# Attention with beacons, then a soft mixture of experts: weight transfers cut into smaller packets, V's conversions and copies moved to other pairs, beacon copies spread over engines

## The chip, the cores and the metric

The kernel runs on one core of one Trainium2 chip. The metric is the device time of one launch in microseconds, the median of several runs. A profile of one execution is read beside it; its times count from the start of the profiled span. Engines are named as in the profile: PE (TensorE matmul), PEld (its weight load), DVE (VectorE), ACT (ScalarE), POOL (GpSimd), SP (SyncE, which only issues transfers here).

## The reference

Queries, keys and values have shape 8 x 8 x 576 x 64 (batches, heads, rows, width), float32. Each head has 16 more keys and values, the beacons, which every query sees; the other keys are causal.

```python
k_all = np.concatenate([beacon_k, k], axis=2)
v_all = np.concatenate([beacon_v, v], axis=2)
scores = scale * np.matmul(q, k_all.transpose(0, 1, 3, 2))
causal[:, Nb:] = np.triu(np.ones((S, S), dtype=bool), k=1)
a = softmax(np.where(causal, -1e9, scores))
attn = np.matmul(a, v_all)
```

The heads of a row are put side by side to x (4608 x 512), and a soft mixture of 8 experts with 4 slots each follows:

```python
logits = x @ phi                                  # 4608 x 32
d = softmax of logits over the 4608 rows
slot_input = d.T @ x                              # 32 slots x 512
slot_out[e] = relu(slot_input[e] @ w1[e]) @ w2[e] # w1 512 x 1024, w2 1024 x 512
out = softmax of logits over the 32 slots @ slot_out
```

## The kernel before

**Pairs.** Two heads are one pair; four pairs are one batch, and the kernel walks 32 pairs, n = 0 to 31. For each pair it has a list of words (`order` and `lists`, lines 544 to 560), written out by hand, and `do` (L571) emits each word's instructions. Every engine takes its instructions in that order, so the lists set the order of the work on all of them. `order[n % 4]` is the list of the steady pairs; below, "list 4k" means one with n % 4 = 0.

**Words.** `S0` to `S3` score a pair in four steps (L366 on PE, the exponential at L373 on ACT, masks at L357 on POOL; `S0` belongs to the next pair). `M` is the mask of the first step (L383, DVE). `A0` and `A1` attend for the pair before, one head each (L396, PE); with `A1`, DVE takes reciprocals (L404) and writes xb (L405), which frees the accumulators for the next `A0`. `Qa Qb Ka Kb` transpose q and k of the next two pairs (L345 on PE, copied by DVE at L347); `T` words do the same for a single pair (L330, L332). `X0 X12 X34` transpose xb, `L0 L1` make logits (L457, exponential at L461), `D` transposes the dispatch weights (L496; dT copied at L498 to L500), and `SI` adds a batch to the slot inputs (L525, added to siq at L529). `BC` and `BT` cast and transpose the beacons of batches 1 to 7 (L305, L310, copies at L320).

**V.** A batch's values come by two transfers of 128 partitions x 2 rows (`load_r`) in packets of 512 bytes, a small one of beacon values into the first of these tiles (`load_bv`), and two for the last rows (`load_vl`). `c0 c1` convert them to 16 bits (L411, POOL in steady lists), `cl` the last rows (L428, four POOL instructions), and `d0 d1` copy the first 64 partitions to a second, padded tile vd (L421, DVE), which `attend` reads. The tiles vh and vd exist twice, by batch.

**Loads.** SP issues q, k and V in program order, q and k six pairs ahead into five buffers each, in packets of 2304 bytes. The weights are issued by POOL (L191), cast from 32 to 16 bits on the way: 27 whole pieces of 1 MB (read) and ten halves. `worder` takes w1 and w2 of experts 0 to 3 first, then w1 of experts 4 to 7, then their w2. How many pieces have been issued by pair n is `want(n)` (L628); the issue stands ahead of `S0`, and in the last pair ahead of `D`. A whole piece is 256 rows of w1 or 512 rows of w2; partition p reads two or four neighbouring rows in one run of 8192 bytes. So a tile's partitions hold every second row of x's width (or every fourth of the hidden width), and the operands that meet the weights are taken with the same stride (`every2`, L503, and `turn`, L736).

**Tail.** After the last pair the slot sums, layer 1 (L725), relu (L732, L734), `turn` (L741, copied at L744 into a padded tile that POOL clears at L702), and layer 2 (L752) follow. Only then are the outputs made (L792, scaled at L794 and L797) and stored.

Of the kernel before, what the change touches and what calls it, by code (L numbers as in the profile page):

```python
# [17 lines left out]
def kernel(  # L18
# [153 lines left out]
    NPC = 4 * E  # L172
    NV = NW + 3
# [7 lines left out]
    def load_w(x):  # L181
        if x < NV:
            m, hs = worder[x], (0, 1)
            t = (wh if x < NW else vrp).tile([P, 2048], F16, name="w", tag="w" if x < NW else "vr")
        else:
            m, hs = worder[NV + (x - NV) // 2], ((x - NV) % 2,)
            t = qkp.tile([P, J * P], F16, name="wx", tag=homes[x - NV])
        e, r = divmod(m, 4)
        w = moe_w1[e, r * 256:(r + 1) * 256] if r < 2 else moe_w2[e, (r - 2) * 512:(r - 1) * 512]
        src = w.rearrange("(p s) f -> p (s f)", p=P)  # L190
        nc.gpsimd.dma_start(out=t[:, 0:1024 * len(hs)],  # L191
                            in_=src[:, 1024 * hs[0]:1024 * (hs[-1] + 1)])
        for i, h_ in enumerate(hs):
            wv[(m, h_)] = t[:, 1024 * i:1024 * (i + 1)]
# [83 lines left out]
    EG = 4  # L278
# [28 lines left out]
    def beacon_t(b0, b1, copy=nc.vector.tensor_copy):  # L307
# [6 lines left out]
        for lo, hi in [(0, 2)] if b0 == 0 else [(2, 3), (3, M - 1), (M - 1, M)]:  # L314
            for r in range(2):
# [4 lines left out]
                copy(out=dst[64 * r:64 * r + 64, 2 * lo:2 * hi, :].rearrange(  # L320
# [103 lines left out]
    def cast_vl(b):  # L424
        t = vl.pop(b)
        for r in range(2):
            for i in range(2):
                nc.gpsimd.tensor_copy(  # L428
                    out=vh[b % 2][64 * i:64 * i + UE, 4, H // 2 * r:H // 2 * (r + 1), 0:D],
                    in_=t[64 * r:64 * r + UE, :, D * i:D * i + D])  # L430
# [71 lines left out]

    def every2(t):  # L503
        lo = 2 * P * (t // 2) + t % 2
        return slice(lo, lo + 2 * P - 1, 2)

    def si_piece(b):
        sp = ps_tr.tile([P, NDC, NSL], FP, name="tr", tag="tr")
        for t in range(NDC):
            for i in range(NCH):  # L510
# [3 lines left out]
                    xb[b % 2][0:m, POS[i], :, :].rearrange("p h d -> p (h d)")[:, every2(t)],  # L514
# [17 lines left out]
    def si_turn():  # L532
        sp = ps_tr.tile([P, NDC, NSL], FP, name="tr", tag="tr")
        for t in range(NDC):
            nc.tensor.matmul(sp[:, t, :], siq[:, every2(t)], slc[:, :],
                             start=True, stop=True)
# [7 lines left out]
    order = ["S1 A0 L1 M S2 Qa Qb S3 A1 Ka S0", "S1 D A0 SI M S2 Kb S3 A1 X0 c0 S0",  # L544
             "S1 A0 M S2 Qa Qb S3 A1 X12 d0 c1 S0", "S1 A0 L0 M S2 Ka Kb S3 A1 X34 d1 cl S0"]
# [25 lines left out]
    def do(n, w):  # L571
# [13 lines left out]
        elif w == "BC":  # L585
            beacon_cast(1, B, nc.scalar.copy)
        elif w == "BT":
            beacon_t(1, B, nc.scalar.copy)
# [16 lines left out]
        elif w[0] == "c" or w[0] == "d":  # L605
# [4 lines left out]
            elif w == "cl":  # L610
                cast_vl(vb)
# [24 lines left out]
    beacon_t(0, 1, nc.scalar.copy)  # L636
# [197 lines left out]
```

## Time and profile before

| | |
|---|---|
| median of 3 runs | 205.14 us (203.96 to 206.57) |
| profiled execution, whole time | 206.35 us |
| its span | 204.6 us, mean granted clock 0.939 |
| PE / DVE / ACT / POOL busy | 161.9 / 145.3 / 130.7 / 115.5 us |
| packets of SP's queue | 34375, 38.87 MB, 56.2% of 16 engines' span |
| packets of POOL's queue | 5328, 16.78 MB written, 42.5% |
| whole weight piece, issue to landing | 8.3 us median |
| first weight issue, last weight landing | 29.3 us, 175.8 us |
| layer 2 ends, outputs begin | 176.3 us, 177.7 us |

A packet's size in the profile is what it writes: a weight packet of 4096 bytes has read 8192. A row of instruction groups reads: line, engine, operation, output <- inputs, shapes, count, then busy time and mean duration, and the engine's idle time before them with what ended it. In a timeline the first two columns are start and length in us, neighbouring instructions of one kind are merged with their count (x2), and the bracket at the end is the idle time before and its releaser.

### The profile page before, as it was taken

To read this page: it belongs to the slowest core of one execution; us is meant where nothing else is said; L and a number is where in the kernel's file an instruction comes from. 1 tells how busy PE (TensorE), PEld (TensorE's weight loads), DVE (VectorE), ACT (ScalarE), POOL (GpSimd) and SP (SyncE) were. 2 spreads that over 40 slices of the span, in tenths; PEclk is the share of its full clock that TensorE was granted. 3 is DMA by queue.
4 is the path that set the end of the run, shared out by engine and by line. 5 is a ranking of instruction groups with operands and counts; after the bars stand their busy time and mean duration, and the time that the engine had idled before them with its cause. 6 is when DMAs were issued, how large, how long until landed. Compare 5 with 4: busy or idle time off the path is not lost.

```text
span 204.6 us, 6942 instructions
## 1 busy us (share of the span) xinstructions
PE 161.9 (79%) x2893; PEld 110.5 (54%) x2893; DVE 145.3 (71%) x294; ACT 130.7 (64%) x191; POOL 115.5 (56%) x278
## 2 busy tenths in 40 slices
PE   2669774899999989999898999589999999888000
PEld 2337562667667657667566675367677764332000
DVE  4665589587988989788998898469796624499100
ACT  3574883678788778878777787628868211399000
POOL 7996269347976759754983885169974650000000
PEclk9999999589999999999999999859999999999855
DMA  6999999988999899999999999999999999199995
GB/s 194 311 343 352 333 339 236 243 268 193 321 235 283 285 272 287 239 319 316 304 255 291 338 260 285 257 314 206 214 215 212 186 205 191 39 354 420 416 418 213
DMA packets 39735, 56.09 MB, mean 274 GB/s; under 512 B 4127, under 2 KB 24343, under 8 KB 39703
## 3 DMA queue, kind: packets, MB, share of 16 engines
q1 hardware_dynamic: 34375, 38.87, 56.2%
q0 software_dynamic: 5328, 16.78, 42.5%
q8 instruction: 22, 0.36, 0.6%
q14 instruction: 10, 0.08, 0.1%
HBM read 62.98 MB, written 9.44 MB: 354 GB/s over the span
## 4 chain that ended last, share of the span: by engine, by line
PE 33%; DVE 32%; DMA 11%; POOL 7%; issue 5%; ACT 4%; POOLq 0%; DVEq 0%; SPq 0%
PE av L396 10%; DMA qf<-in_q_dram 8%; DVE xb L405 8%; DVE qT L347 6%; PE sc L366 5%; DVE kT L347 5%; DVE osb L797 4%; DMA kf<-in_k_dram 3%; PE tr L345 3%; ACT ex L373 3%; DVE vd L421 3%; PE tr L457 3%; PE av L752 2%; PE tr L525 1%; DVE siq L529 1%
## 5 line engine op out<-in xcount | busy, mean ns | idle before, releaser
L373 ACT ACTIVATE ex<-sc 128x928 f16<-128x928 f32 (+2 forms) x128 | 106.5, 868 | 34.6 <-PE sc L366 27.5
L357 POOL TENSOR_SCALAR_AFFINE_SELECT ex<-ex 128x256 f16<-128x256 f16 x128 | 52.0, 426 | 38.5 <-ACT ex L373 33.4
L396 PEld LDWEIGHTS <-ex 128*128 128x128 f16 (+1 forms) x960 | 44.1, 110 | 18.2 <-issue 16.0
L366 PE MATMUL sc<-qT,kT 64*64 64x128 bf16 (+3 forms) x640 | 47.5, 270 | 4.9 <-ACT ex L373 2.5
L396 PE MATMUL av<-vh,ex 128*128 128x65 f16 x819 | 44.9, 203 | 0.8 <-POOL ex L357 0.7
L366 PEld LDWEIGHTS <-kT 64*64 64x64 bf16 (+1 forms) x640 | 17.9, 106 | 21.3 <-issue 9.9
L396 PE MATMUL av<-vd,ex 128*128 128x130 f16 x126 | 22.9, 232 | 6.3 <-DVE xb L405 6.0
L405 DVE TENSOR_TENSOR xb<-av,r 128x640 f16<-128x640 f32 (+1 forms) x32 | 26.1, 814 | 1.1
L347 DVE COPY qT<-tr 128x640 bf16<-128x640 bf16 (+1 forms) x24 | 17.5, 770 | 8.2 <-PE tr L345 8.2
L411 POOL CAST vh<-vr 128x1024 f16<-128x1024 f32 x15 | 15.8, 1053 | 8.9 <-DMA vr<-in_beacon_v_dram 8.9
L347 DVE COPY kT<-tr 128x640 bf16<-128x640 bf16 (+1 forms) x24 | 18.0, 771 | 3.8 <-PE tr L345 3.6
L383 DVE TENSOR_TENSOR ex<-ex,fmask 128x672 f16<-128x672 f16 x32 | 17.7, 554 | 0.9 <-ACT ex L373 0.6
L794 ACT ACTIVATE osb<-fp,rc 128x512 f32<-128x512 f32 (+1 forms) x19 | 12.0, 665 | 6.6 <-PE fp L792 6.3
L191 POOL DMA_DIRECT2D w<-in_moe_w_dram x27 | 15.0, 557 | 0.0
L428 POOL CAST vh<-vl 48x256 f16<-48x256 f32 x32 | 14.0, 438 | 1.1
L421 DVE COPY vd<-vh 64x1040 f16<-64x1040 f16 x16 | 13.9, 870 | 0.2
L345 PE MATMUL tr<-idb,kf 128*64 128x128 bf16 x216 | 10.4, 227 | 3.0 <-DVE qT L347 3.0
L797 DVE TENSOR_SCALAR osb<-fp,rc 128x512 f32<-128x512 f32 x18 | 12.3, 745 | 0.6 <-PE fp L792 0.6
L792 PE MATMUL fp<-soh,eLh 128*128 128x512 f16 (+1 forms) x37 | 10.8, 371 | 2.2 <-DVE soh L777 0.6
L345 PE MATMUL tr<-idb,qf 128*64 128x128 bf16 x216 | 9.4, 230 | 2.8 <-DMA qf<-in_q_dram 2.8
L442 PE MATMUL tr<-idh,xb 128*128 128x128 f16 (+1 forms) x140 | 11.4, 223 | 0.2 <-DVE kT L332 0.2
L447 DVE COPY xT<-tr 128x512 f16<-128x512 f16 (+1 forms) x21 | 10.5, 502 | 0.4 <-PE tr L442 0.4
(110 smaller groups left out, 176.7 us busy)
## 6 DMA issues: line engine op xcount, KB each, us to landing
w<-in_moe_w_dram POOLq DMA_DIRECT2D x27, 512.0 KB, 8.3
qf<-in_q_dram SPq DMA_DIRECT2D x32, 288.0 KB, 7.5
kf<-in_k_dram SPq DMA_DIRECT2D x32, 288.0 KB, 6.1
out_dram<-osb SPq DMA_DIRECT2D x16, 512.0 KB, 6.0
vr<-in_v_dram SPq DMA_DIRECT2D x15, 512.0 KB, 6.2
wx<-in_moe_w_dram POOLq DMA_DIRECT2D x10, 256.0 KB, 10.2
vl<-in_v_dram SPq DMA_DIRECT2D x16, 96.0 KB, 6.4
out_dram<-osb SPq DMA_DIRECT2D x3, 256.0 KB, 2.6
```

Of the source, the lines that this page charges most:

```text
L191: nc.gpsimd.dma_start(out=t[:, 0:1024 * len(hs)], in_=src[:, 1024 * hs[0]:1024 * (hs[-1] + 1)])
L345: nc.tensor.transpose(tp[64 * r:64 * r + 64, j - j0, :], ts[r][:, j, :].bitcast(BF)[:, 1::2], idb[:, :])
L347: nc.vector.tensor_copy(out=dst[:, :, Nb:Nb + S].rearrange("p a (s j) -> p a s j", j=J)[:, :, :, j0:j1], in_=tp[:, :, :].rearrange("p j (a ...
L357: nc.gpsimd.affine_select(out=x, in_=x, compare_op=AL.is_ge, fill=0.0, base=base, pattern=pattern, channel_multiplier=cm)
L366: nc.tensor.matmul(sc[p0:p0 + kn, a, col:col + un], kT[n // 2 % 2][64 * a:64 * a + 64, n % 2, k0:k0 + ks * (kn - 1) + 1:ks], qT[n // 2 % 2 ...
L373: nc.scalar.activation(x[:, :, o:o + w], sc[:, :, 0:w], AF.Exp, scale=scale)
L383: nc.vector.tensor_tensor(out=x, in0=x, in1=fmask[:, :].unsqueeze(1).broadcast_to([P, 2, XT + UL]), op=AL.min)
L396: nc.tensor.matmul(dst, ex[n][0:kn, a, o:o + m], rhs, start=j in first, stop=j in final)
L405: nc.vector.tensor_tensor(out=xb[b % 2][:, :, h0:h0 + dh * (na - 1) + 1:dh, :].rearrange("p i a d -> p a i d"), in0=avv[:, :, :, 0:D], in1 ...
L411: eng.tensor_copy(out=vh[b % 2][:, 2 * r:2 * r + 2, :, 0:D].rearrange("p s h d -> p h s d"), in_=vr.pop((b, r))[:, :, :].rearrange("p h (s ...
L421: nc.vector.tensor_copy(out=vd[b % 2][64 * r:64 * r + 64, :, r, :, :], in_=vh[b % 2][0:64, 2 * r:2 * r + 2, :, :])
L797: nc.vector.tensor_scalar(out=osb[:, j - j0, :], in0=fp_[:, :], scalar1=rc[:, i:i + 1], scalar2=None, op0=AL.mult)
```

## The change

Four edits, made together.

- **Packets.** All w1 pieces and the w2 pieces of experts 0 to 3 are read with neighbouring rows on neighbouring partitions, so a partition reads two runs of 4096 bytes (w1) or four of 2048 bytes (w2). w2 of experts 4 to 7 stays as it was. The operands that meet the changed pieces are taken without a stride.
- **Pace.** `want` grows by 0.68 pieces a pair instead of 0.8, with new values for pairs 25 to 30.
- **V.** `c1` moves among the lists, `cl` is split into `e0` and `e1` (two POOL instructions each) at two places of list 4k+3, and `d0 d1` stand in list 4k, behind `A1`. `Ka` leaves list 4k for 4k+1, just ahead of `Kb`, and `X0` moves from 4k+1 to 4k+2. The lists of the first and last pairs are rewritten alike; `c0` and `c1` of batch 1 move ahead to lists 2 and 3.
- **Beacons.** The casts of `BC` go from ACT to POOL; of the six copies of `BT`, three stay on ACT and three go to DVE.

```diff
@@ load_w
         w = moe_w1[e, r * 256:(r + 1) * 256] if r < 2 else moe_w2[e, (r - 2) * 512:(r - 1) * 512]
-        src = w.rearrange("(p s) f -> p (s f)", p=P)
-        nc.gpsimd.dma_start(out=t[:, 0:1024 * len(hs)],
-                            in_=src[:, 1024 * hs[0]:1024 * (hs[-1] + 1)])
+        if r < 2 or e < EG:
+            src = w.rearrange("(s p) f -> p s f", p=P)
+            nc.gpsimd.dma_start(out=t[:, :].rearrange("p (s f) -> p s f", f=w.shape[1]), in_=src)
+        else:
+            src = w.rearrange("(p s) f -> p (s f)", p=P)
+            nc.gpsimd.dma_start(out=t[:, 0:1024 * len(hs)],
+                                in_=src[:, 1024 * hs[0]:1024 * (hs[-1] + 1)])
@@ beacon_t
-    def beacon_t(b0, b1, copy=nc.vector.tensor_copy):
+    def beacon_t(b0, b1, copies=(nc.vector.tensor_copy,) * 2):
...
-                copy(out=dst[64 * r:64 * r + 64, 2 * lo:2 * hi, :].rearrange(
+                copies[r](out=dst[64 * r:64 * r + 64, 2 * lo:2 * hi, :].rearrange(
@@ cast_vl
-    def cast_vl(b):
-        t = vl.pop(b)
-        for r in range(2):
-            for i in range(2):
-                nc.gpsimd.tensor_copy(
-                    out=vh[b % 2][64 * i:64 * i + UE, 4, H // 2 * r:H // 2 * (r + 1), 0:D],
-                    in_=t[64 * r:64 * r + UE, :, D * i:D * i + D])
+    def cast_vl(b, r):
+        t = vl[b]
+        for i in range(2):
+            nc.gpsimd.tensor_copy(
+                out=vh[b % 2][64 * i:64 * i + UE, 4, H // 2 * r:H // 2 * (r + 1), 0:D],
+                in_=t[64 * r:64 * r + UE, :, D * i:D * i + D])
@@ si_piece, si_turn
-                    xb[b % 2][0:m, POS[i], :, :].rearrange("p h d -> p (h d)")[:, every2(t)],
+                    xb[b % 2][0:m, POS[i], :, :].rearrange("p h d -> p (h d)")[:, P * t:P * t + P],
...
-            nc.tensor.matmul(sp[:, t, :], siq[:, every2(t)], slc[:, :],
+            nc.tensor.matmul(sp[:, t, :], siq[:, P * t:P * t + P], slc[:, :],
@@ lists
-    order = ["S1 A0 L1 M S2 Qa Qb S3 A1 Ka S0", "S1 D A0 SI M S2 Kb S3 A1 X0 c0 S0",
-             "S1 A0 M S2 Qa Qb S3 A1 X12 d0 c1 S0", "S1 A0 L0 M S2 Ka Kb S3 A1 X34 d1 cl S0"]
+    order = ["S1 A0 L1 M S2 Qa Qb S3 A1 d0 d1 S0", "S1 D A0 SI M S2 Ka Kb S3 A1 c0 S0",
+             "S1 A0 M S2 Qa Qb S3 A1 X0 X12 c1 S0", "S1 A0 L0 M S2 e0 Ka Kb S3 A1 X34 e1 S0"]
...
-    lists[0] = "S2 M bv S3 S0 c1 d0 d1 cl".split()
+    lists[0] = "S2 M bv S3 S0 c1 d0 d1 e0 e1".split()
     lists[1] = "S1 S2 S3 M T2 A0 A1 S0".split()
-    lists[2] = "S1 A0 M S2 T3 A1 S3 S0 BC".split()
-    lists[3] = "S1 A0 BT M S2 T4 A1 c0 S3 T5 d0 S0 c1".split()
-    lists[4] = "d1 S1 A0 M S2 Qa Qb S3 A1 Ka cl S0".split()
-    lists[5] = "S1 A0 M S2 Kb S3 A1 X0 S0".split()
-    lists[6] = "S1 A0 M S2 Qa Qb S3 A1 X12 c0 S0".split()
-    lists[7] = "S1 A0 L0 M S2 Ka Kb S3 c1 A1 X34 d0 cl S0 d1".split()
-    lists[NP - 4] = "S1 A0 L1 M S2 Ta Tb S3 A1 S0".split()
+    lists[2] = "S1 A0 M S2 T3 A1 S3 S0 BC c0".split()
+    lists[3] = "S1 A0 BT M S2 T4 A1 S3 c1 T5 S0".split()
+    lists[4] = "e0 e1 S1 A0 M S2 Qa Qb S3 A1 d0 d1 S0".split()
+    lists[5] = "S1 A0 M S2 Ka Kb S3 A1 c0 S0".split()
+    lists[NP - 4] = "S1 A0 L1 M S2 Ta Tb S3 A1 d0 d1 S0".split()
@@ do
-            beacon_cast(1, B, nc.scalar.copy)
+            beacon_cast(1, B, nc.gpsimd.tensor_copy)
         elif w == "BT":
-            beacon_t(1, B, nc.scalar.copy)
+            beacon_t(1, B, (nc.scalar.copy, nc.vector.tensor_copy))
@@ want
         if n < 25:
-            return max(0, int(0.8 * n - 1.1))
-        return {25: 20, 26: 22, 27: 24, 28: NV, 29: NV + 4, 30: NV + 4}.get(n, NV + NH)
+            return max(0, int(0.68 * n - 0.6))
+        return {25: 17, 26: 19, 27: 22, 28: 24, 29: NV, 30: NV + 2}.get(n, NV + NH)
@@ turn
-            lo = 4 * P * (t // 4) + t % 4
-            nc.tensor.matmul(tp[:, t, :], hs[:, lo:lo + 4 * P - 3:4], ssel[:, gr, :],
+            lo, st = (4 * P * (t // 4) + t % 4, 4) if gr else (P * t, 1)
+            nc.tensor.matmul(tp[:, t, :], hs[:, lo:lo + st * (P - 1) + 1:st], ssel[:, gr, :],
                              start=True, stop=True)
```

More of the change, by code (lines that the diff above doesn't have):

```diff
@@ L172 @@
     NPC = 4 * E
+    EG = 4
     NV = NW + 3
@@ L275 @@
     slc = const.tile([P, NSL], FP, name="slc")
-    EG = 4
     ssel = const.tile([P, E // EG, EG * SPE], F16, name="ssel")
@@ L500, in dt_piece @@
         nc.vector.memset(dT[b][0:Nb, 0, :], 0.0)
-    def every2(t):
-        lo = 2 * P * (t // 2) + t % 2
-        return slice(lo, lo + 2 * P - 1, 2)
     def si_piece(b):
@@ L604, in do @@
             cast_bv0()
-        elif w[0] == "c" or w[0] == "d":
+        elif w[0] in "cde":
             vb = 0 if n < 2 else b if g == 0 else b + 1
@@ L609, in do @@
                 pass
-            elif w == "cl":
-                cast_vl(vb)
+            elif w[0] == "e":
+                cast_vl(vb, int(w[1]))
             elif w[0] == "c":
@@ L635 @@
     transp(0, 1)
-    beacon_t(0, 1, nc.scalar.copy)
+    beacon_t(0, 1, (nc.scalar.copy,) * 2)
     beacon_k_in(0, nc.vector)
```

## The prediction, made blind

> **What bounds the kernel now.** I read the page's slices first, then the queues, then the stretches.
>
> ```profile
> DMA  6999999988999899999999999999999999199995
> ...
> q1 hardware_dynamic: 34375, 38.87, 56.2%
> q0 software_dynamic: 5328, 16.78, 42.5%
> ```
>
> The transfer engines are busy in every slice but one, and the two queues' packets fill 98.7% of the span. Next, the stretches; the columns are start:end, length, five engines' busy time (count), granted clock, DMA share, GB/s.
>
> ```profile
> 30.00:50.00 20.00, 16.13 (x281) 11.61 (x281) 15.82 (x29) 12.67 (x17) 11.89 (x29) 0.83 0.91 239
> 50.00:95.00 45.00, 41.84 (x801) 29.48 (x799) 39.39 (x81) 36.78 (x53) 31.93 (x76) 1.00 1.04 277
> 95.00:130.00 35.00, 31.75 (x615) 22.45 (x611) 31.58 (x60) 27.59 (x40) 24.72 (x59) 1.00 1.08 292
> 136.00:163.00 27.00, 25.84 (x492) 19.24 (x491) 21.46 (x48) 18.62 (x29) 21.31 (x50) 0.95 1.05 211
> ```
>
> Consecutive packets of one engine overlap, so full is about 1.06. Only 30 to 50 us and a few us near 70 lie below it: some 4 us of empty transfer time before the last weight lands at 175.8. Outputs start only when layer 2 is done (176.3). So the loads are one nearly solid block, and PE, 92% busy beside it, is the second limit. The chain of waits shows where the two meet:
>
> ```profile
> 109.46 0.34 PE tr L345 x8
> 110.00 6.96 DMA kf<-in_k_dram
> 117.03 16.53 DMA qf<-in_q_dram
> 133.60 1.17 PE tr L345 x17
> ```
>
> A q load takes 16.5 us instead of the median 7.5, and PE's transposes of pair 26 start 4 us late. In the packet records of 118.5 to 119.5 us, 46 weight packets alternate with 86 V packets: a V packet (512 bytes, 27 ns) waits behind a weight packet (8192 bytes read, 324 ns) at each turn.
>
> The demand: q, k, v and beacons are 56.2% of 204.6 less 23.1 for output, 91.9 us of packets over 32 pairs, 2.87, by the overlap 2.7 us a pair. Weight DMAs land 2.49 us apart when alone (142.13 to 162.06 in eight steps); at 0.8 a pair that is 2.0. Together 4.7 us a pair, against four pairs in 17.25 us (L405 starts 62.42 and 79.67), 4.31 each. The debt grows until V and q run late at pair 25.
>
> **The change, part by part.**
>
> *Pace and packets.* At 0.68 a pair the weights need 1.69 us, in all 4.4 us a pair. Packets become 16 (w1) or 32 (first half of w2) per engine and piece, from 8. Their price: the ten half pieces of the trace already read 4096 bytes per packet and land 1.25 us apart, twice that being 2.50 against 2.49, so w1 costs nothing. A packet reading 2048 bytes is not in the trace. The records give 324 ns for 8192 and 173 for 4096 bytes, 22 ns more per cut if nothing overlaps; the spacing gives 0. There are 16 x 8 + 8 x 24 = 320 extra packets an engine: 0 to 7.0 us. I take 5 ns, 1.6 us, since the 512-byte rows show 8 ns over their bytes' time (27 against 18.8) before overlap; below 0 no row points. It lies before pair 25 and is hidden in the transfer time that the slower pace frees; without that cover it is added whole. [...]
>
> A q or V packet now waits 154 or some 80 ns instead of 306 per turn, so the loads stay ahead: I remove the stall at pair 25, seen on POOL as 5.32 us before V's conversion at 134.69, after which pair 25's weights are issued (135.68). Unstalled that issue would stand at 130.4.
>
> *Issue on POOL.* 0.547 us for a whole piece, 0.550 for a half, both 128 packets; more packets per issue are not in the trace for POOL. On SP, 1024 packets (V) take 0.38, 128 (q) 0.33. Ends: nothing, or in proportion (1.1 and 2.2 us). I take SP's, the nearest row with a different count: 0.6 us, hidden in POOL's 13 us idle of the 45 above.
>
> *Early lists.* The casts of the beacons leave ACT (2 x 0.57 us) for POOL (1024 columns take 1.05, so 448 about 0.5 each, in a POOL gap of 1.95), and three of six copies go to DVE (0.47 + 2 x 0.18, in a DVE gap of 1.75). PE waited 1.12 us for those ACT copies; I count 1.1 saved, 0 to 1.1. Larger is this:
>
> ```profile
> 30.00 3.46 DVE L421 COPY vd<-vh 64x1040 f16<-64x1040 f16 x2
> 33.49 0.58 DVE L383 TENSOR_TENSOR ex<-ex,fmask 128x672 f16<-128x672 f16 x1
> 34.00 1.44 DVE L347 COPY qT<-tr 128x640 bf16<-128x640 bf16 x2
> ```
>
> Two copies of median 0.52 take 3.46 us while POOL converts and masks without a pause; PE waited 2.99 us for qT. With `d0 d1` moved behind xb of that list, xb of pair 3 starts near 32.5 instead of 35.57: 3.1 us saved, 2 to 3.5. Early: 4.2 us. The same collision in pairs 18 and 22 (2.00 and 1.54 us instead of about 0.45) made those pairs 0.86 and 0.39 us longer; 1.25 more is saved.
>
> *Steady lists.* Here the change costs. In the timeline of DVE from list 20 to list 21:
>
> ```profile
> 106.68 0.82 DVE L405 TENSOR_TENSOR xb<-av,r 128x640 f16<-128x640 f32 x1
> 107.42 0.82 DVE L347 COPY kT<-tr 128x640 bf16<-128x640 bf16 x1
> 108.16 0.22 DVE L498 COPY dT<-tr 128x128 f16<-128x128 f16 x1
> 109.20 0.69 DVE L529 SCALAR_TENSOR_TENSOR siq<-tr,siq 128x512 f32<-128x512 f32 x1 [0.70 <-PE tr L525]
> 110.22 0.72 DVE L347 COPY kT<-tr 128x512 bf16<-128x512 bf16 x1
> 111.08 0.82 DVE L405 TENSOR_TENSOR xb<-av,r 128x640 f16<-128x640 f32 x1
> ```
>
> Between two xb stand Ka's copy, the dT copies, a wait for PE, siq, the mask, Kb's copy. Now `d0 d1` (0.43 + 0.52) stand where Ka stood (0.82) and Ka's copy comes after the mask, where nothing hides it: +0.13 and +0.74 (0.82 less the 0.08 overlap), 0.87 us a batch; the old Ka slot, beside PE's attend, is filled by the copies. xb frees the accumulators for PE's next attend, so the 4.40 us segment becomes 5.27. The other three segments lose `X0`, `d0`, `d1` from a DVE that waits 0.3 to 0.7 us for PE's transposes in each, and gain nothing. In a list 4k+3 POOL's `e0` (2 x 0.44) goes ahead of the last mask, which slides from 66.90 to about 67.8; its products come 0.3 us into the attend at 67.77: nothing, at most 0.1. Five such segments before pair 25: +4.35 us. A pair is now 18.12 / 4 = 4.53 us, above the 4.4 that the transfers need.
>
> The contiguous slices of xb, siq and hs leave the instructions; the spread of their weight loads (L512 97 ns, L741 117) bounds that at 0.2 us either way.
>
> *The tail.* Pair 25's issue: 130.4 - 4.2 - 1.25 + 4.35 = 129.3. From there the queue is never empty. Before, 14 whole pieces were left; 135.68 + 14 x 2.49 + 2.0 of q and k gives 172.5, and the last landing was 175.81, so 3.3 for start and stragglers. Now want(24) is 15, so 17 pieces are left: 129.3 + 17 x 2.49 + 2.8 (pair 31 and most of 30, at 1.4 each) + 3.3 = 177.7. PE's own tail, some 6 us earlier, then waits for the late w2 halves. **Sum: +1.9 us**: the time won before pair 25 is less than the 7.5 us of weights put behind it. A check: transfer work is unchanged but for 1.6 us, and idle grows from some 4 to about 5.
>
> The profiled execution took 206.35 around its span of 204.6; the sum gives 208.25. The median of the runs shown is 1.21 lower, so I predict **207.0**. A measurement of this kernel tells about 2% (201.0 to 209.2) from no change.
>
> **The rivals.**
>
> *Loads at their floor (18%).* If Ka's copy is hidden after all, pair 25 comes 4 us earlier, transfers bind throughout and only empty time can go: 4.1 less 1.6, so 202.6. For it: DVE has waits in each segment. Against: they are for PE's transposes, not behind the mask.
>
> *POOL's issue grows with the packets (17%), slower.* With 2.2 us for a w2 piece, one issue stands ahead of the masks of the next pair's S1. A block of `cl`, issue and copy (67.26 to 69.78, 2.5 us) held PE up by nothing. `c1` or `c0` or `e1` plus 2.2 plus 0.2 is 3.3 to 3.45, about 0.9 too long, in seven of eight w2 pieces: 6 us, 213.0. It decides from an issue of about 1.3 us. For it: no row of POOL's has another count of packets; against: SP's rows.
>
> *Packets at full price (10%).* At 22 ns the first sixteen pieces cost 0.35 more, 0.24 a pair: 4.64 exceeds 4.53, a debt of 2.2 us by pair 25, and 1.2 more on w1 afterwards: 210.4.
>
> *The cuts don't share the engine (7%).* If a queue keeps the engine for a group of packets, smaller ones change no turn; the stall of 4.1 stays: 211.1. The alternation in the records speaks against it. [...]
>
> **How the numbers follow.** The forecast has 48%, mostly between 204.5 and 209.5 by the ends of the early gain and the packet price. Range 202.3 to 212.5: from the floor to just under the POOL rival. Faster 0.05 (the part of the floor case below its bound), same 0.58, slower 0.37 (34% of three rivals, 3% of the forecast's edge).
>
> **What will show it.** L347's wait on q gone, POOL's wait before V's conversion under 1 us; vd copies at 0.4 to 0.6 us; xb to xb 5.2 us once a batch, else as now; issue of w at 0.6 us; the last wx landing near 178 with PE waiting for it. Wrong if the 5.2 us is missing, if POOL's issue exceeds 1.3 us, or if loads still run late.

## The result, and the profile after

The changed kernel takes **215.24 us** (median of 4 runs, 213.31 to 216.08) against 205.06 (203.96 to 206.57) for the kernel before on the same chip: a ratio of 1.048, 95% interval 1.038 to 1.058. It is slower by 10 us; I had predicted 207.0, in a range that ended at 212.5. The profiled execution took 216.08, its span is 214.4 (206.35 and 204.6 before). Ratios, here and below, leave out executions more than 1.5% longer than the shortest of their kernel (the profiled ones of issue_moved and early_between, below, are such); medians keep them.

The page of the changed kernel, its slices and its queues:

```profile
PEclk9999999599999979988997999999799999979955
DMA  6999999979999999999799999899999999489995
...
q1 hardware_dynamic: 34375, 38.87, 54.0%
q0 software_dynamic: 10448, 16.78, 44.8%
```

The row of transfers has two 7s and an 8 ahead of the last weights, where it had three 8s. The packets of the two queues still cover 98.8% of the span, though it is 9.8 us longer, because the records of POOL's queue add up to more (44.8% of 214.4 is 96.1 us, 87.0 before). The row above it is one that I had not read before: the clock granted to PE, in tenths of full speed. It shows dips, three of them 20.5 us apart (74.2, 94.7 and 115.2 us). The kernel before has this row, with dips near 36 and 132 us and at the end:

```profile
PEclk9999999589999999999999999859999999999855
```

The same stretches as before (start:end, length, busy time and count of PE, PEld, DVE, ACT and POOL, granted clock, DMA share, GB/s):

```profile
30.00:50.00 20.00, 17.08 (x292) 12.21 (x289) 15.08 (x31) 13.67 (x19) 14.66 (x33) 0.83 0.98 244
50.00:95.00 45.00, 38.68 (x716) 27.42 (x716) 34.80 (x72) 32.88 (x48) 29.51 (x69) 0.96 1.05 266
95.00:130.00 35.00, 31.51 (x559) 22.03 (x555) 26.92 (x51) 25.23 (x37) 22.43 (x51) 0.91 1.03 260
136.00:163.00 27.00, 24.32 (x475) 17.62 (x474) 20.60 (x42) 19.55 (x28) 21.08 (x45) 0.94 1.01 189
```

Between 50 and 95 us PE did 716 matmuls instead of 801, DVE 72 operations instead of 81: the attention itself is slower, not the loads. The granted clock is 0.96 and 0.91 in the steady stretches where it was 1.00. What PE waits for has changed hands; the list of its waits (total us, times, longest):

```profile
PE av L400 <- DVE vd L425: 8.7, 7, 1.6
PE av L400 <- DVE xb L409: 4.6, 13, 0.6
```

In the kernel before, the first of these rows does not exist, and the second is this:

```profile
PE av L396 <- DVE xb L405: 6.0, 19, 0.6
```

The timeline of DVE over the boundary from list 20 to list 21, where I had counted the cost of the steady lists:

```profile
112.07 0.82 DVE L409 TENSOR_TENSOR xb<-av,r 128x640 f16<-128x640 f32 x1
112.81 1.02 DVE L425 COPY vd<-vh 64x1040 f16<-64x1040 f16 x2
113.86 0.22 DVE L501 COPY dT<-tr 128x128 f16<-128x128 f16 x1
...
115.17 0.69 DVE L527 SCALAR_TENSOR_TENSOR siq<-tr,siq 128x512 f32<-128x512 f32 x1 [0.95 <-PE tr L523]
115.78 0.50 DVE L387 TENSOR_TENSOR ex<-ex,fmask 128x672 f16<-128x672 f16 x1
116.28 1.45 DVE L351 COPY kT<-tr 128x640 bf16<-128x640 bf16 x2
118.31 0.22 DVE L408 RECIPROCAL r<-av 128x10 f32<-128x10 f32 x1 [0.57 <-PE av L400]
118.56 0.82 DVE L409 TENSOR_TENSOR xb<-av,r 128x640 f16<-128x640 f32 x1
```

From xb to xb it is 6.49 us, against 4.40 before and 5.27 predicted. The order is the one I had counted; the time lies elsewhere. PE waits 1.23 us for the two copies into vd before it can attend, and from 115.2 to 118.6 its clock is at half, so that DVE then waits for the slot sums (L523) and for `av`.

The end, in the chain of waits (start, length, what):

```profile
163.03 12.37 DMA wx<-in_moe_w_dram
175.41 0.28 issue
175.69 9.74 DMA wx<-in_moe_w_dram
```

The last weights land at 185.4 and layer 2 ends at 185.9; before it was 175.8 and 176.2. So the tail has the form that I predicted, and it starts late: pair 25's weights are issued at 138.6 instead of the 129.3 of my sum. The whole miss is there.

### The profile page after: what moved, and what is told of

It reads as the page before. It is cut to its first block, busy times and chain, and to the rows that moved or that the text cites. A ratio compares the mean times of both kernels' runs of the same rounds, so it can differ in the third digit from the quotient of the medians.

```text
span 214.4 us, 6954 instructions
## 1 busy us (share of the span) xinstructions
PE 167.3 (78%) x2893; PEld 112.6 (53%) x2893; DVE 141.9 (66%) x297; ACT 129.1 (60%) x186; POOL 120.3 (56%) x280
## 3 DMA queue, kind: packets, MB, share of 16 engines
q0 software_dynamic: 10448, 16.78, 44.8%
## 4 chain that ended last, share of the span: by engine, by line
DVE 34%; PE 33%; DMA 10%; POOL 7%; issue 6%; ACT 3%; POOLq 0%; DVEq 0%
PE av L400 11%; DMA wx<-in_moe_w_dram 10%; DVE xb L409 9%; DVE qT L351 7%; PE sc L370 6%; DVE kT L351 6%; PE tr L349 5%; PE tr L460 4%; DVE osb L793 3%; DVE xT L450 3%; DVE vd L425 3%; ACT ex L377 2%; PE tr L523 2%; DVE r L408 2%; PE fp L788 2%
## 5 line engine op out<-in xcount | busy, mean ns | idle before, releaser
L361 POOL TENSOR_SCALAR_AFFINE_SELECT ex<-ex 128x256 f16<-128x256 f16 x128 | 52.9, 429 | 49.4 <-ACT ex L377 42.9
L370 PE MATMUL sc<-qT,kT 64*64 64x128 bf16 (+3 forms) x640 | 48.5, 273 | 6.1 <-ACT ex L377 3.0
L351 DVE COPY qT<-tr 128x640 bf16<-128x640 bf16 (+1 forms) x24 | 17.5, 770 | 8.3 <-PE tr L349 8.3
L351 DVE COPY kT<-tr 128x640 bf16<-128x640 bf16 (+1 forms) x24 | 17.4, 769 | 8.0 <-PE tr L349 7.8
L387 DVE TENSOR_TENSOR ex<-ex,fmask 128x672 f16<-128x672 f16 x32 | 18.5, 579 | 1.6 <-ACT ex L377 1.5
L193 POOL DMA_DIRECT2D w<-in_moe_w_dram x24 | 17.6, 734 | 0.0
L788 PE MATMUL fp<-soh,eLh 128*128 128x512 f16 (+1 forms) x37 | 12.0, 424 | 2.1 <-ACT osb L790 1.4
L793 DVE TENSOR_SCALAR osb<-fp,rc 128x512 f32<-128x512 f32 x18 | 12.6, 747 | 1.3 <-PE fp L788 1.1
L431 POOL CAST vh<-vl 48x256 f16<-48x256 f32 x32 | 12.7, 397 | 1.3
L445 PE MATMUL tr<-idh,xb 128*128 128x128 f16 (+1 forms) x140 | 10.4, 215 | 0.7
L349 PEld LDWEIGHTS <-kf 128*64 128x64 bf16 x216 | 8.3, 125 | 3.4 <-issue 3.0
L460 PE MATMUL tr<-xT,phih 128*128 128x288 f16 x56 | 9.2, 286 | 0.6 <-DVE xT L450 0.2
```

The costliest lines, as they stand in the source:

```text
L193: nc.gpsimd.dma_start(out=t[:, :].rearrange("p (s f) -> p s f", f=w.shape[1]), in_=src)
L349: nc.tensor.transpose(tp[64 * r:64 * r + 64, j - j0, :], ts[r][:, j, :].bitcast(BF)[:, 1::2], idb[:, :])
L351: nc.vector.tensor_copy(out=dst[:, :, Nb:Nb + S].rearrange("p a (s j) -> p a s j", j=J)[:, :, :, j0:j1], in_=tp[:, :, :].rearrange("p j (a ...
L361: nc.gpsimd.affine_select(out=x, in_=x, compare_op=AL.is_ge, fill=0.0, base=base, pattern=pattern, channel_multiplier=cm)
L370: nc.tensor.matmul(sc[p0:p0 + kn, a, col:col + un], kT[n // 2 % 2][64 * a:64 * a + 64, n % 2, k0:k0 + ks * (kn - 1) + 1:ks], qT[n // 2 % 2 ...
L387: nc.vector.tensor_tensor(out=x, in0=x, in1=fmask[:, :].unsqueeze(1).broadcast_to([P, 2, XT + UL]), op=AL.min)
```

## The experiments

All kernels were compared with runs of the kernel before on the same chip. The table has what the text uses: the segment from xb of pair 4k-1 to xb of pair 4k in the steady batches (k = 2 to 6), the issue of pair 25's weights, the whole pieces not yet issued then (two halves count as one), the last landing of a weight and the time between the two, in us. The three kernels with the new packets and the old lists have 4.54 to 4.56 at pair 8 and 4.40 after it.

| kernel | segment | pair 25's issue | pieces left | last landing | from issue to landing | median | ratio (95%) |
|---|---|---|---|---|---|---|---|
| before | 4.40 | 135.7 | 14 | 175.8 | 40.1 | 205.06 | 1 |
| after | 5.55 to 6.77 | 138.6 | 17 | 185.4 | 46.8 | 215.24 | 1.048 (1.038 to 1.058) |
| lists_alone | 5.55 | 133.8 | 14 | 174.5 | 40.7 | 208.78 | 1.011 (1.005 to 1.017) |
| packets_pace | 4.40 | 128.0 | 17 | 175.0 | 47.0 | 205.91 | 0.998 (0.996 to 1.001) |
| packets_alone | 4.40 | 132.5 | 14 | 177.9 | 45.4 | 208.41 | 1.012 (1.007 to 1.017) |
| pace_alone | 4.40 | 128.4 | 17 | 175.0 | 46.6 | 205.96 | 1.003 (1.000 to 1.007) |
| dups_back | 4.76 | 131.4 | 17 | 178.5 | 47.1 | 209.11 | 1.013 (1.010 to 1.016) |
| fill | 5.55 to 5.75 | 134.0 | 17 | 180.7 | 46.7 | 212.54 | 1.037 (1.029 to 1.045) |
| issue_moved | 5.55 to 6.55 | 137.8 | 17 | 184.9 | 47.1 | 214.08 | 1.033 (1.023 to 1.044) |
| old_pace | 5.76 to 6.69 | 139.6 | 14 | 181.6 | 42.0 | 211.52 | 1.031 (1.024 to 1.040) |
| beacons_alone | 4.40 | 132.3 | 14 | 172.6 | 40.3 | 205.80 | 1.001 (0.997 to 1.004) |
| pace_between | 4.40 | 127.8 | 16 | 172.4 | 44.6 | 204.18 | 0.993 (0.990 to 0.997) |
| early_between | 4.40 | 127.2 | 16 | 172.5 | 45.3 | 202.33 | 0.982 (0.977 to 0.988) |
| early_packets | 4.40 | 127.7 | 16 | 173.7 | 46.0 | 204.64 | 0.998 (0.994 to 1.002) |

The six kernels with 17 pieces left need 46.6 to 47.1 us from that issue to the last landing, whatever came before. (With 14 left it is 40.1 to 42.0, and 45.4 in packets_alone, where two later pairs still wait for loads.) So with 17 pieces left the time of a kernel is the time of that issue plus a nearly fixed tail, and what has to be explained is what comes before it.

### The lists and beacons alone

The changed kernel with the old packets and the old pace.

```diff
-        if r < 2 or e < EG:
-            src = w.rearrange("(s p) f -> p s f", p=P)
...
+        src = w.rearrange("(p s) f -> p (s f)", p=P)
...
-            return max(0, int(0.68 * n - 0.6))
-        return {25: 17, 26: 19, 27: 22, 28: 24, 29: NV, 30: NV + 2}.get(n, NV + NH)
+            return max(0, int(0.8 * n - 1.1))
+        return {25: 20, 26: 22, 27: 24, 28: NV, 29: NV + 4, 30: NV + 4}.get(n, NV + NH)
```

> The new lists and beacon copies with the old packets and the old pace. Theory L (the lists cost the time: the attend of a batch's first pair waits for d0 d1, which stand directly ahead of it, some 1.2 us in seven batches, PE's clock is granted at half for 3.4 us after such a wait, and X0 beside X12 makes a third segment 0.35 us longer): the pairs are as slow as in the changed kernel (17 us or more... 18.7 to 20 us for four pairs), the stall on q at pair 25 is gone since slower pairs need fewer bytes per us, and the tail is the old one: 209 to 213 us. Rival W (packets, pace and the longer issue on POOL cost the time, lists cost little): 203 to 206 us, four pairs in 17.3 to 18.1 us.

Measured: ratio 1.011. Each steady batch has the segments 3.93, 4.80, 4.45 and 5.55, with a granted clock of 1.0 from 37.5 to 167.2 us. PE's waits in this kernel:

```profile
PE av L396 <- DVE vd L421: 8.3, 7, 1.8
```

So the lists bring the wait for vd by themselves, 1.07 us in each steady batch, and with it 5.55 instead of 4.40. They don't bring the 6.5 to 6.8 of the changed kernel: with the same lists the clock stays up here, against theory L, and the time is just under its 209 to 213. This trace is of an execution of 208.08 us with a mean granted clock of 0.955; two of the other three had 0.936 and 0.937 and took 209.49 and 210.10, so the clock may have fallen in some of their batches, which no trace shows.

The lists' 1.011 and the 0.998 of the packets with the pace (next run) don't add up to 1.048. The table shows two reasons. With the new lists pair 25's issue stands near 134 us at either pace while the clock stays up (133.8 here, 134.0 in fill), so the slower pace wins nothing there and still leaves three more pieces behind it: the last landing is 174.5 here and 180.7 in fill. Of the other 4.7 us, to the 185.4 of the changed kernel, 2.8 lie in pairs 8 to 25, where its clock drops (82.2 us, 79.4 in fill), and 1.8 ahead of pair 8.

### The packets and the pace alone

The kernel before with the packets and `want` of the change.

```diff
@@ before
+        if r < 2 or e < EG:
+            src = w.rearrange("(s p) f -> p s f", p=P)
...
-            return max(0, int(0.8 * n - 1.1))
+            return max(0, int(0.68 * n - 0.6))
```

> The new packets and the new pace with the old lists and beacon copies. Theory L: pairs as in the kernel before (17.25 us for four), no stall at pair 25, pair 25's weights issued near 130 us, and seventeen pieces behind it: last weight near 178, 205 to 208 us. Rival W: 212 us or more, with slower pairs or loads that run late.

Measured: ratio 0.998. No pair waits for a load, four pairs take 17.25 us from pair 8 to pair 24, pair 25's weights are issued at 128.0 and the attention ends 6.6 us sooner than before. The stretches of this kernel, to be put beside those of after:

```profile
50.00:95.00 45.00, 41.97 (x807) 29.54 (x806) 39.31 (x80) 36.64 (x53) 33.58 (x78) 1.00 1.10 292
95.00:130.00 35.00, 32.47 (x637) 23.34 (x634) 30.61 (x62) 28.72 (x41) 25.63 (x59) 1.00 1.10 291
```

807 matmuls at a full clock where after has 716. The 17 pieces behind pair 25 take back what was won: last landing 175.0, against 175.8.

### The packets alone, and the pace alone

```diff
@@ packets_alone: before with the packets of the change, want as before
@@ pace_alone: before with
-            return max(0, int(0.8 * n - 1.1))
+            return max(0, int(0.68 * n - 0.6))
```

> The new packets alone, old pace, old lists. Theory L: pairs as before, q and V land sooner, the stall at pair 25 is 0 to 2 us instead of 4, the transfers stay full and the end is bound by their total: 202 to 205 us. Rival W: smaller packets cost transfer time (up to 7 us) or POOL time: 207 us or more.

> The kernel before with the new pace alone, packets of 8192 bytes read. Theory P (what keeps q and V in time is the slower pace, not the packet size): no stall on q, k or V over 1 us, attention ends within 1.5 us of packets_pace (155.8), time 204 to 207 us. Rival Q (the packet size does it): a stall of 2 us or more in pairs 17 to 28, attention ends at 158 us or later.

Measured: packets alone 1.012 (208.41 us, where theory L had 202 to 205), and stalls are there, if at other pairs: the steps from pair 17 to 18 and from 26 to 28 take 7.92, 8.93 and 7.78 us, and with the pace alone 4.47, 4.44 and 4.78. Pace alone 1.003, no stall, four pairs in 17.25 us, as theory P had it. So the stalls go with the pace, not with the packets. The median q load takes 7.6 us with the packets alone (7.5 before), 6.1 with the pace alone and 6.6 with both: smaller packets did not let q through sooner.

### The copies into vd put back

The changed kernel with `d0 d1` of batches 2 to 7 in lists 4k+2 and 4k+3 again; `Ka` stays where the change put it.

```diff
-    order = ["S1 A0 L1 M S2 Qa Qb S3 A1 d0 d1 S0", "S1 D A0 SI M S2 Ka Kb S3 A1 c0 S0",
-             "S1 A0 M S2 Qa Qb S3 A1 X0 X12 c1 S0", "S1 A0 L0 M S2 e0 Ka Kb S3 A1 X34 e1 S0"]
+    order = ["S1 A0 L1 M S2 Qa Qb S3 A1 S0", "S1 D A0 SI M S2 Ka Kb S3 A1 c0 S0",
+             "S1 A0 M S2 Qa Qb S3 A1 X0 X12 d0 c1 S0", "S1 A0 L0 M S2 e0 Ka Kb S3 A1 X34 d1 e1 S0"]
```

> The changed kernel with d0 and d1 of batches 2 to 7 back in lists 4k+2 and 4k+3 (the lists of pair 4 keep theirs); Ka stays in 4k+1. Theory L: PE no longer waits for vd ahead of the attend of a batch's first pair and its clock stays full, so that segment falls from 5.6 to 6.8 us to 5.0 or less; pair 25's weights are issued 6 to 9 us sooner: 207 to 210 us. Rival K (Ka behind the mask is what makes the segment long, not the wait for vd): the segment stays above 5.3 us and the whole falls by 3 us at most.

Measured: ratio 1.013, 6 us less than the changed kernel. The same boundary on DVE's timeline, now 4.77 us:

```profile
89.51 0.82 DVE L409 TENSOR_TENSOR xb<-av,r 128x640 f16<-128x640 f32 x1
90.26 0.21 DVE L501 COPY dT<-tr 128x128 f16<-128x128 f16 x1
...
91.67 0.69 DVE L527 SCALAR_TENSOR_TENSOR siq<-tr,siq 128x512 f32<-128x512 f32 x1 [1.08 <-PE tr L523]
92.28 0.50 DVE L387 TENSOR_TENSOR ex<-ex,fmask 128x672 f16<-128x672 f16 x1
92.70 1.44 DVE L351 COPY kT<-tr 128x640 bf16<-128x640 bf16 x2
94.04 0.20 DVE L408 RECIPROCAL r<-av 128x10 f32<-128x10 f32 x1
94.28 0.82 DVE L409 TENSOR_TENSOR xb<-av,r 128x640 f16<-128x640 f32 x1
```

PE has no wait for vd left in the steady lists, and the clock is 1.0 from 43.5 to 163.0 us. Two copies of 0.41 to 0.62 and 0.43 us, moved two lists and one list nearer to their reader, cost 6 us. `Ka` behind the mask costs 4.76 - 4.40 = 0.36 a batch, less than the 0.74 I had given it.

### PE kept busy during the wait

The clock dips could be a cause or only a sign. So the wait was left and filled: five matmuls into a spare tile, whose result is not used, between `D` and `A0` of lists 4k+1 from pair 9 to pair 25.

```diff
-"S1 D A0 SI M S2 Ka Kb S3 A1 c0 S0",
+"S1 D W A0 SI M S2 Ka Kb S3 A1 c0 S0",
...
+        elif w == "W":
+            if n >= 8:
+                idle_work(ps_tr.tile([P, 512], FP, name="tr", tag="tr"), 5)
```

> The changed kernel with five idle 512-column matmuls between D and A0 in the lists 4k+1 (pairs 9, 13, 17, 21, 25), where PE waits 1.07 to 1.28 us for vd. They add work that the result does not use. Theory G (the wait itself costs 1.1 us, and in four of the batches PE's granted clock then falls to half for 3.4 us, 1.0 to 1.3 us more each): the clock stays at 1.0 in those batches, their segments are all near 5.6 us instead of 6.5 to 6.8, pair 25's weights are issued 3 to 4 us sooner, 210.5 to 212.5 us in all. Rival S (something else makes those batches slow, say POOL's longer issue or late masks): they stay at 6.5 us or more and the time within 1.5 us of the changed kernel's.

Measured: ratio 1.037, with more work than the changed kernel and 2.7 us less time; the two intervals overlap a little, and 1.8 us of the gain stand ahead of pair 8, where there is no filler, so the clock is the firmer evidence. First two neighbouring windows of the changed kernel, the wait of list 13 in the first of them, then two of this kernel, where the filler of the same list runs from 71.0 to 72.3:

```profile
70.80:74.20 3.40, 2.03 (x45) 1.51 (x42) 3.30 (x7) 2.88 (x4) 2.18 (x5) 1.00 1.08 342
74.20:77.60 3.40, 3.40 (x40) 2.02 (x39) 1.57 (x6) 0.90 (x1) 0.48 (x2) 0.50 1.14 273
```

```profile
69.00:72.50 3.50, 3.31 (x52) 1.99 (x48) 3.40 (x8) 2.91 (x4) 2.25 (x5) 1.00 1.06 339
72.50:75.90 3.40, 3.16 (x57) 1.97 (x54) 2.45 (x7) 1.71 (x2) 0.82 (x3) 1.00 1.13 275
```

In the changed kernel PE was busy 2.03 of 3.40 us, and the next window runs at a clock of 0.50. With the filler it was busy 3.31 of 3.50, and the next window runs at 1.00. The clock stays at 1.0 from 31.5 to 147.6 us and drops in the batch at the end that has no filler; that segment is 7.57 (6.81 in the changed kernel), those with filler 5.55 to 5.75. So the dips are a cause: of the 6.5 to 6.8 us about 1 is the clock.

### The weights' issue moved away from the copy, and the old pace

Two kernels for the question why the wait of the changed kernel is 1.23 to 1.29 us and not the 1.07 of lists_alone. In the first, POOL issues the weights of the lists 4k ahead of `S3` instead of `S0`; the second is the changed kernel with the old `want`.

```diff
@@ issue_moved
-            if w == "S0" or n == NP - 1 and w == "D":
+            if w == ("S3" if n % 4 == 0 and n >= 8 else "S0") or n == NP - 1 and w == "D":
@@ old_pace
-            return max(0, int(0.68 * n - 0.6))
+            return max(0, int(0.8 * n - 1.1))
```

> The changed kernel with the weights' issue of the lists 4k (n = 8 and on) ahead of S3 instead of ahead of S0, so that POOL is done with it before d0 starts. Theory G with the collision (an issue of 0.71 us instead of 0.55 is still running when d0 starts, d0 takes 0.57 to 0.62 instead of 0.41, the wait grows from 1.07 to 1.23 us or more, and only then does the clock fall): d0 at 0.41, waits at 1.07, no drop in pairs 12 to 20, segments at 5.55, 210.5 to 212.5 us. Rival S: d0 shorter, but the clock falls in the same batches, 214 us or more.

> The changed kernel with the old pace (0.8 a pair and the old numbers for pairs 25 to 30). Theory T (the three pieces put behind pair 25 hold up layer 2): last weight 4 to 7 us earlier against the last xb, 2 to 4 us off the time, 211 to 213 us, if loads are not late again; pairs as in the changed kernel. Rival D (at 0.8 a pair q and V run late even with small packets, as in packets_alone): stalls of 3 us or more on q, k or V, 214 us or more.

Measured: 1.033 and 1.031. First the two engines in the changed kernel, POOL and then DVE, each on its own timeline, at list 12:

```profile
72.61 0.76 POOL L193 DMA_DIRECT2D w<-in_moe_w_dram  x1
```

```profile
72.24 0.82 DVE L409 TENSOR_TENSOR xb<-av,r 128x640 f16<-128x640 f32 x1
72.98 1.07 DVE L425 COPY vd<-vh 64x1040 f16<-64x1040 f16 x2
```

And in lists_alone, with the old packets:

```profile
71.17 0.55 POOL L192 DMA_DIRECT2D w<-in_moe_w_dram  x1
```

```profile
70.80 0.82 DVE L405 TENSOR_TENSOR xb<-av,r 128x640 f16<-128x640 f32 x1
71.54 0.87 DVE L421 COPY vd<-vh 64x1040 f16<-64x1040 f16 x2
```

In both the copies begin 0.37 us into the issue. The issue of the new packets takes 0.71 to 0.76, the pair of copies 1.02 to 1.07; with the old packets it takes 0.55, the copies 0.87. In the changed kernel's lists 8 and 24 no weight is issued there, and the first copy takes 0.41, the wait is 1.07. In issue_moved all steady first copies take 0.41 to 0.42 and all waits are 1.08; in old_pace, which issues in other lists, the wait is 1.23 to 1.28 in those lists and 1.08 in the one without an issue (pair 20). So the longer issue is what lengthens the copy, by its end: in packets_pace a copy at 62.63 us that lies whole beside the first 0.46 us of an issue of 0.72 takes 0.41.

The clock doesn't follow the wait so closely. In issue_moved, with waits of 1.08, it dropped in two of the steady batches and stayed up in three (segments 6.55 and 6.22, and 5.55 three times), where lists_alone with 1.07 has no drop in five. The traced execution took 215.84 us at a mean clock of 0.908; another of the four took 211.27 at 0.943, so its batches may be those that theory G forecast, but no trace of it was kept. In old_pace the batch of pair 20 dropped after a wait of 1.08 (segment 6.52) and that of pair 16 did not after 1.28 (5.76). So the longer issue accounts for the longer wait, but whether it accounts for the drops stays open.

old_pace answers its own question as theory T had it: the last weight lands 12.6 us behind the last xb, where it is 17.5 in the changed kernel, no pair waits for a load, and the time is 211.52.

Beside the issue of the new packets the copies lose 0.15 to 0.20 us (1.02 to 1.07 for the pair instead of 0.87), though 0.34 to 0.39 us of the issue are left when they begin. Beside the old issue, with 0.18 us left, they lose nothing (0.87 in lists_alone, as in lists 8 and 24 of the changed kernel). What in the issue holds the copy up, no run here shows.

### The beacon copies alone

```diff
@@ before
-            beacon_cast(1, B, nc.scalar.copy)
+            beacon_cast(1, B, nc.gpsimd.tensor_copy)
...
-            beacon_t(1, B, nc.scalar.copy)
+            beacon_t(1, B, (nc.scalar.copy, nc.vector.tensor_copy))
```

> The kernel before with the beacon edit alone: casts on POOL, three of the six copies on DVE. Theory (the two engines' copies into one tile go one after the other, and DVE's mask and q copy stand behind them): pair 1 to pair 2 takes 6.4 to 6.7 us instead of 6.02, the copies last 1.7 us in all, as on ACT alone, each waiting for the other engine's; the time stays within 1%, since the loads have slack to lose 0.5 us there. The rival, as I predicted it: the copies run side by side, pair 1 to pair 2 takes 4.9 to 5.1 us.

Measured: ratio 1.001, pair 1 to pair 2 takes 6.61 us as in the changed kernel, 6.02 before. ACT and then DVE, in this kernel:

```profile
24.48 0.18 ACT L320 COPY bkT<-tr 64x32 bf16<-64x32 bf16 x1 [0.76 <-PE tr L310]
24.90 0.47 ACT L320 COPY bkT<-tr 64x384 bf16<-64x384 bf16 x1 [0.24 <-DVE bkT L320]
25.80 0.18 ACT L320 COPY bkT<-tr 64x32 bf16<-64x32 bf16 x1 [0.43 <-DVE bkT L320]
```

```profile
24.69 0.18 DVE L320 COPY bkT<-tr 64x32 bf16<-64x32 bf16 x1 [2.13 <-ACT bkT L320]
25.41 0.36 DVE L320 COPY bkT<-tr 64x384 bf16<-64x384 bf16 x1 [0.54 <-ACT bkT L320]
26.01 0.18 DVE L320 COPY bkT<-tr 64x32 bf16<-64x32 bf16 x1 [0.24 <-ACT bkT L320]
...
26.76 0.76 DVE L332 COPY qT<-tr 128x576 bf16<-128x576 bf16 x1
```

The two engines take turns, each waiting for the other's copy into the same tile: 24.48 to 26.19, 1.71 us, against 1.74 for all six on ACT alone. And DVE's mask and copy of q now stand behind them: qT begins at 26.76 instead of 25.43. What I had not expected is the next pair: it is 5.65 instead of 7.64, in which the copies into vd, 0.4 us later, take 1.45 us instead of 3.46.

### Toward a better kernel

What the runs left standing: the kernel before with a pace between the two, and the early lists mended without the wait for vd.

```diff
@@ pace_between: before with
-            return max(0, int(0.8 * n - 1.1))
-        return {25: 20, 26: 22, 27: 24, 28: NV, 29: NV + 4, 30: NV + 4}.get(n, NV + NH)
+            return max(0, int(0.74 * n - 0.85))
+        return {25: 18, 26: 20, 27: 23, 28: 25, 29: NV + 1, 30: NV + 3}.get(n, NV + NH)
@@ early_between: that, and
-    lists[2] = "S1 A0 M S2 T3 A1 S3 S0 BC".split()
-    lists[3] = "S1 A0 BT M S2 T4 A1 c0 S3 T5 d0 S0 c1".split()
-    lists[4] = "d1 S1 A0 M S2 Qa Qb S3 A1 Ka cl S0".split()
+    lists[2] = "S1 A0 M S2 T3 A1 S3 S0 BC c0".split()
+    lists[3] = "S1 A0 BT M S2 T4 A1 S3 c1 T5 S0".split()
+    lists[4] = "S1 A0 M S2 d0 d1 Qa Qb S3 A1 Ka cl S0".split()
@@ early_packets: that, and the packets of the change
```

> The kernel before with a pace of 0.74 pieces a pair (0.8 before, 0.68 after), and 18, 20, 23, 25, 28, 30 pieces by pairs 25 to 30. Theory: at 0.74 the demand is 2.7 + 0.74 x 2.49 = 4.54 us a pair against 4.31 that the pairs take, a debt of 0.23 a pair in place of 0.38, so the stall at pair 25 falls from 4.1 to some 1.5 us or vanishes, and two pieces fewer stand behind pair 25 than at 0.68: last weight landing between 172 and 175 us, 203 to 206 us in all. Rival (the transfers are one solid block whatever their order): last landing 175 to 176 and the time within 0.5% of before.

> pace_between with the conversions of batch 1's V moved one pair ahead and its two copies into vd put behind the mask of pair 4, away from POOL's conversions; beacons and steady lists as before. Theory: pairs 2 to 4 take some 3 us less (7.64 + 4.99 become 4.1 + 5.5), the loads and weights are issued that much sooner, and transfer time that lay empty between 30 and 50 us is filled: last weight 1 to 3 us sooner than in pace_between, 201 to 204 us. Rival (solid block): no more than 0.5 us.

> early_between with the packets of 2048 and 4096 bytes. Theory (the pace, not the packet, sets the stall, and POOL's longer issue is hidden in these lists): as early_between, within 0.5%. Rival (smaller packets bring q and V sooner): the stall left at pair 25 in early_between is gone and the time 1 to 2 us less.

Measured: 0.993, 0.982 and 0.998. pace_between came out as forecast, without a stall at pair 25. **early_between is the fastest of all**, 202.33 us (200.30 to 203.50), though its interval (0.977 to 0.988) leaves open whether that is a full 2%. Its steps from pair 2 to pair 4 take 5.32 and 3.49 us instead of 7.64 and 4.99, and the row of transfers in its page (that execution took 203.50 us, the longest of six) has no 8 left before the last weights:

```profile
DMA  5999999999999999999999999999999998199994
```

The last weight lands no sooner than in pace_between (172.5 in an execution of 203.50 us, 172.4 in one of 203.16); the medians differ by 1.85 us, and where those went no trace here shows. With the new packets on top it takes 2.3 us more, which neither theory nor rival had: q loads take 7.9 us in the median instead of 7.0, and POOL waits 5.8 us for loads ahead of V's conversions instead of 1.8. Where the transfers are solid, the small packets have a price; how much of it is POOL's longer issue is not separated.

## Why the prediction was wrong, by its steps

The spans differ by 9.8 us, and I had predicted 1.9: pair 25's issue came 9.3 later than in my sum, the tail was 1.6 shorter.

**"The old Ka slot, beside PE's attend, is filled by the copies": the step that failed.** I put the cost of the copies in that place at 0.13 us, and PE's wait for them at nothing. I followed DVE from xb to xb and asked whom each copy keeps from running. I did not ask who reads vd. `A0` of list 4k+1 attends for the first pair of the new batch, so it needs the copies that the change puts right in front of it; before, they stood one and two lists earlier. PE waits 1.07 to 1.28 us for them, and in the steady batches that is 5.55 - 4.76 = 0.79 us a batch above what `Ka` costs, by lists_alone and dups_back; the drops of the clock behind the wait come on top. None of my rivals named this wait.

**The clock of PE was no term of the sum.** PE's idle time was counted as its length. In the records, the granted clock goes to 0.50 for a window of 3.41 us, sometimes for two, mostly after a window in which PE was busy for less than about 0.65 of it. In the traces of the kernel before and of the changed one, all its changes lie on a grid of such windows: in the changed kernel at 36.67, 43.49, 74.21, 77.63, 94.69 and 98.11 us, for example, 2, 9, 1, 5 and 1 windows apart. Over the fourteen kernels, of windows between 28 and 172 us at full clock, 28 of 32 with a share below 0.63 were followed by a drop, 4 of 11 between 0.63 and 0.66, 6 of 498 above. Five of these six had PE busy for over 95%, all between 154 and 168 us, with some 35 matmuls of a single column (L681 in the kernel before) in them, so the busy share is not all that counts. In lists_alone, with waits of 1.07 us, the emptiest windows of the steady batches stand at 0.656; in the changed kernel, with 1.23 to 1.28, at 0.60 to 0.61. How much of a wait falls into one window also depends on where the grid lies: issue_moved has two windows at 0.655 that were followed by a drop and one that was not, with one length of wait. In the changed kernel each drop costs 0.9 to 1.2 us of segment (6.49 to 6.77 against 5.55). PE was far from idle in the windows that cost the changed kernel its clock from pair 12 to 20: it was busy for 0.60 to 0.61 of them.

**"POOL's issue: I take SP's, 0.6 us."** It takes 0.71 to 0.76 with two or four times the packets, inside the two ends and far under the 1.3 from which my rival decided. My rival was wrong about who pays: not the masks behind the issue on POOL, but the DVE copy beside it, by 0.15 to 0.20 us. That this is what tips the clock is argued from the shares above and not shown.

**"0.87 us a batch" for `Ka` behind the mask.** Of this, 0.74 was `Ka`; dups_back shows 0.36. The size was off, and in the other direction.

**X0 beside X12.** I let `X0` leave list 4k+1 for nothing. The segment after it went from 4.46 to 4.80 in every kernel with the new lists, 0.34 a batch. The chain of the changed kernel runs through it:

```profile
122.49 0.82 DVE xb L409
123.32 0.94 DVE xT L450 x2
124.26 0.04 issue
124.30 0.65 PE tr L460 x4
124.95 0.30 PE sc L370 x2
125.25 0.42 PE tr L349 x10
```

Two copies instead of one stand ahead of the logits (`L0`), and those ahead of the scores and of the transposes of k. POOL, which has `e0` in the same segment, is not in this chain. That was read from traces; `X0` alone was not moved.

**"Early: 4.2 us."** Little of it came: from xb of pair 1 to that of pair 7, ahead of the first steady batch, it is 31.4 us, 32.2 before. The collision of the copies with POOL's conversions did go (pair 2 to 3: 4.07 instead of 7.64, 4.5 predicted). The gain was eaten by the beacon copies taking turns (6.61 where I had 4.9), by the wait for vd in list 4 (1.56 us; pair 3 to 4 takes 6.20 instead of 4.99), and by the two steps from pair 4 to pair 6, 0.64 and 0.33 longer. That the 4 us were there to be had is shown by early_between: 27.7 us for the same pairs.

**"The stall at pair 25 removed."** It is gone, but not for my reason. I had the smaller packets let q and V through; pace_alone removes it with the old packets, and packets_alone has stalls at pairs 18, 27 and 28. The base of 130.4 for the unstalled issue was 2.0 to 2.4 too late (128.4 and 128.0); 1.25 of that I had taken off for the collisions in pairs 18 and 22, which went with the pace, too. Whether an engine's turns changed at all with the smaller packets is left open: the records as kept (46 and 86 in one us) don't name the engine, so the turns that I read from them are not shown, and the landing of q did not get shorter in any of the three pairs of kernels that differ by the packets.

**The packets' price, "1.6 us, hidden".** Hidden, yes: packets_pace and pace_alone have the same last landing (175.0). Where the cover is gone it is 2.3 us (early_packets against early_between; packets_alone against before has 1.2%, some 2.5 us), a little over the 1.6 (320 packets an engine at 5 ns, an estimate; 2.3 us would be 7 ns each) and far under 7.0, though the records of POOL's queue grew by 7.7 us of an engine's time (46.5% of 204.1 against 42.8% of 203.8), about the upper end. Records that grow and a landing that doesn't: most of it overlapped. The 18.8 ns that I set against the 27 of a 512-byte packet is what its bytes take by the rows of SP's queue, 13 ns at 128 bytes and 159 at 4096.

**The tail.** 48.4 predicted, 46.8 measured; a further piece costs 2.0 to 2.2 us there (40.1 for 14, 44.6 for 16, 46.6 for 17), not 2.49.

**The sum again with the measured terms**, for pair 25's issue: against packets_pace, where the lists are those of before, xb of pair 8 comes 1.7 us later and the pairs from 8 to 25 take 82.2 us instead of 72.9, 9.3 more. These are four segments of 6.77, 6.70, 6.49 and 5.55 in place of 4.40 (7.9), and four times 0.34 (1.4). Of the 7.9, 1.4 are `Ka`, 3.2 the wait for vd and 3.3 the clock. I had 3.48 for these four. Against my sum the steady batches came to 10.4 us instead of 4.35 (five segments up to pair 24, and `X0`), and the early part won 0.8 instead of 4.2: these two, 6.1 and 3.4, are the 9.3 but for 0.2. The rival with the floor named 202.6; early_between takes 202.3 with the old packets and other lists, which doesn't show that this is a floor, since its executions go down to 200.3.

## What to carry to other kernels

When work is moved in a hand-written order, ask of each moved copy who reads its result first and how far away that reader now is; two copies put one and two lists nearer cost 6 us here. Count PE's idle time twice: as its length, and, where it brings PE's busy share of a window of 3.41 us under about 0.65, as a likely stretch at half clock behind it (here 3.41 us at 0.50, after 28 of 32 windows with a share below 0.63). A batch near the edge is fragile: at 0.655, two windows of issue_moved were followed by a drop and one was not. And where transfers set the end, what a slower pace leaves for later has to be paid for by a stall that it removes: here it was with the old lists, and not with the new ones, where there was none left to remove.

## What the hardware showed that I had not expected

- A clock of 0.50 for 3.41 us after a window with PE 60% busy, with an edge at a share near 0.65 that has exceptions on both sides; with five added matmuls in each wait of 1.07 to 1.28 us the clock stayed up.
- An issue by POOL of 256 or 512 packets takes 0.71 to 0.76 us against 0.55 for 128, so neither constant nor in proportion; a DVE copy beside the end of such an issue takes 0.57 to 0.62 instead of 0.41.
- Copies by two engines into parts of one tile ran strictly in turn, each waiting for the other engine's: 1.71 us for six, 1.74 on one engine. That the parts don't overlap did not help.
- Packets of 2048 and 4096 bytes read did not bring the other queue's q loads sooner, and cost 2.3 us where the transfers were solid.
